# Cluster attention and spatial gating on one core: for batches 1 to 3 the mean of the values is formed on all partitions by one matmul and added by POOL, in place of flag and mean rows in the value product

## The chip, the cores and the metric

The kernel runs on one core of one Trainium2 chip. The metric is the device time of one execution in microseconds. The core has TensorE (PE in the profile, with its weight loads as PEld), VectorE (DVE), ScalarE (ACT), GpSimd (POOL), SyncE (SP, which here only issues DMAs), and 16 DMA engines. Each engine works through its own instructions in the order in which they were written out, and waits on semaphores for the others.

## The reference, cut to what matters

There are 4 batches, 8 heads, 768 positions, 64 elements a head and 16 clusters a head. Every query and key is given to the cluster whose centroid has the largest cosine with it; a query sees only the keys of its own cluster. A gated MLP follows that mixes over positions.

```python
mask = q_assign[:, :, :, None] == k_assign[:, :, None, :]
scores = scale * np.matmul(q, k.transpose(0, 1, 3, 2))
scores = np.where(mask, scores, -1000000000.0)
attn = np.exp(scores - np.max(scores, axis=-1, keepdims=True))
attn = attn / (np.sum(attn, axis=-1, keepdims=True) + 1e-09)
x = np.matmul(attn, v)                     # then heads side by side: (4, 768, 512)
h = np.maximum(x @ w_in, 0.0)              # w_in: 512 x 1024
u, v = h[..., :512], h[..., 512:]
v_n = (v - mean(v)) / np.sqrt(var(v) + 1e-06)
v_s = np.einsum('ts,bsd->btd', w_spatial, v_n) + b_spatial[None, :, None]
out = (u * v_s) @ w_out                    # w_out: 512 x 512
```

One case matters for this change: a query whose cluster holds no key. All its scores are then the same -1e9, its softmax is uniform, and its row of the output is the mean of all 768 values of that head.

## The kernel before, in words

Numbers that need more than one f16 are kept as a high and a low f16 part, so a product is made of three matmuls (high by high, high by low, low by high). Heads are treated in pairs: 4 batches of 4 pairs, so pair numbers n run from 0 to 15 and `NPR` is 4. The 768 positions are 6 tiles of 128.

`prep(n)` loads keys, queries and values of a pair, splits them (L527, L529 for queries and keys, L592, L593 for the values), finds the clusters (logits L544 to L546, then five DVE passes L557 to L562), and puts the one-hot rows of the clusters, scaled to a large penalty, under the queries and keys, so that the mask is part of the score matmul. It also forms the sum of the values over all positions: 12 matmuls with a matrix of ones (L600, L601) add the high and low parts of the six tiles, DVE takes the sum apart again into high and low (L609, L610), ACT scales the low part (L611), and two DMAs (L612, L613) put both as one row each (rows 81 and 82) into the tile `mean`.

`shifts(n)` computes the scores once to get each query's largest score (L641, reduced by DVE at L648), takes the negated maximum `nl` (L659), and lets ACT write three columns from it: the shift (L660) and two flag columns (L663), the second one scaled by a power of two. A flag is 1 for a query without a key in its cluster and 0 for the others. A DMA transpose (L664) and a DMA (L665) put the three as rows 80 to 82 under the queries.

`attend(n)` goes through two heads of six key tiles. For each key tile PE makes the scores (L685, L687), ACT the exponential (L691) and its high part (L693), POOL the low part (L694), and PE adds 18 matmuls of 65 or 64 columns to the accumulator `av` (L699). At the first key tile of a head six more matmuls go ahead of these: they multiply rows 0 to 82 of the queries with `mean`, so that flagged queries get the mean of the values, and the sum that belongs to it in column 64. Then DVE divides (L718 to L720, the result is `xn`), ACT makes the high part (L722), POOL the low part (L723), and a DMA transpose (L725) brings the pair to `xT`.

`mlp(b)` does the gated MLP of a batch: 324 matmuls of 128x512 a batch, all on one line (L743), with the normalisation on DVE and POOL (L764 to L785), gating (L804 to L806), a DMA transpose (L807) and the output. Its work is mixed with the attention of the batch behind it; the MLP of the last batch has no attention beside it.

The order of the work on each engine isn't written by hand. `Plan.run` simulates the engines once when the kernel is built: each operation carries an estimated duration, a due time (`DUE` for pairs of batch 0, `DUE_M` for later ones) and an offset to it (`K_SC`, `K_EXP` and the like), and the ready operation with the least due time plus offset goes next. Durations and offsets thus set only the order; the chip then takes its own time. Weights for the MLP are loaded and split in the same way (`weights`, L447 to L476), w_in early and w_spatial and w_out during batch 1.

## Time and profile before

| what | value |
|---|---|
| median of 3 runs | 699.76 us (699.73 to 700.55) |
| the profiled execution's own time | 698.77 us |
| its span, first to last instruction | 697.0 us |
| granted TensorE clock, mean | 0.998 |
| busy: PE, DVE, ACT, POOL | 637.2, 472.6, 434.7, 426.1 us |

A row of a grouping view reads: line, engine, operation, out<-in, shape, count | busy us, mean ns of one | idle us of the engine just before them, and what ended that idle time. A row of the waits reads: who waited for whom: us in total, times, longest us. A row of the table by stretches gives each engine's busy time in that stretch with its count of instructions. The time of an execution is a little longer than the span, which runs from the first to the last instruction.

### The profile page before, as it was taken

The numbers are of one execution on the slowest core, as the hardware profiler recorded it, in microseconds if no ns is written. First come the engines' busy times: TensorE is split into PE (matmuls) and PEld (weight loads), VectorE is DVE, ScalarE is ACT, GpSimd is POOL, SyncE is SP. The second block draws the span as 40 slices with busy tenths as digits, with TensorE's granted clock in tenths as the row PEclk, the third lists the DMA queues.
The fourth block names the chain that finished last, engine by engine and source line by source line (L and its number), as shares of the span: only waits on it lengthen the run. The fifth ranks groups of instructions, "written<-read, shape, count | busy, mean of one in ns | idle before, by whom it ended". The sixth has DMA issues, their size and how long they took to land.

```text
span 697.0 us, 16953 instructions
## 1 busy us (share of the span) xinstructions
PE 637.2 (91%) x6871; PEld 382.3 (55%) x6871; DVE 472.6 (68%) x933; ACT 434.7 (62%) x679; POOL 426.1 (61%) x296
## 2 busy tenths in 40 slices
PE   2578879989998898999999999999989999999997
PEld 1246656666546555566555656566555656544443
DVE  6989899996898989648687846748586732115220
ACT  2349999998587837569565956769465766612111
POOL 1027979988777936568557866658456857723311
PEclk9999999999999999999999999999999999999999
DMA  5475745676534675255421538345221123230123
GB/s 163 129 178 126 223 104 135 153 130 145 150 80 134 133 162 141 53 159 107 138 52 25 142 69 167 71 97 94 58 52 25 36 44 54 62 84 1 31 60 91
DMA packets 107322, 70.71 MB, mean 101 GB/s; under 512 B 91182, under 2 KB 93932, under 8 KB 107244
## 3 DMA queue, kind: packets, MB, share of 16 engines
...
q14 instruction: 24, 0.20, 0.1%
...
## 4 chain that ended last, share of the span: by engine, by line
PE 51%; DVE 23%; ACT 7%; DMA 7%; issue 5%; POOL 5%; SPq 1%; POOLq 0%; ACTq 0%; DVEq 0%
PE acc L743 30%; DVE nm L648 11%; PE acc L699 8%; PE sc L687 4%; PE sc L685 4%; PE acc L641 3%; POOL pt L694 3%; ACT p L691 3%; DMA gT<-ghl 2%; ACT pt L693 2%; DVE lo L529 1%; DVE y L778 1%; DVE v L783 1%; DMA raw<-in_kqT_dram 1%; DVE wsp L457 1%
## 5 line engine op out<-in xcount | busy, mean ns | idle before, releaser
L694 POOL TENSOR_TENSOR pt<-p,pt 128x768 f16<-128x768 f32 x192 | 327.8, 1722 | 123.6 <-ACT pt L693 91.7
L691 ACT ACTIVATE p<-sc,plog 128x768 f32<-128x768 f32 x192 | 169.0, 897 | 59.8 <-PE sc L687 51.7
L648 DVE TENSOR_REDUCE nm<-acc 128x1 f32<-128x512 f32 (+1 forms) x288 | 179.8, 683 | 4.4 <-PE acc L641 4.2
L693 ACT CAST pt<-p 128x768 f16<-128x768 f32 x192 | 156.0, 828 | 10.1 <-PE acc L699 8.3
L699 PEld LDWEIGHTS <-pt 128*128 128x128 f16 x3456 | 125.7, 98 | 33.4 <-POOL pt L694 8.1
L699 PE MATMUL acc<-vhl,pt 128*128 128x65 f16 (+1 forms) x3456 | 135.3, 194 | 6.6 <-POOL pt L694 6.4
L743 PE MATMUL acc<-win,xT 128*128 128x512 f16 x576 | 129.7, 379 | 0.3 <-DVE nm L648 0.2
L641 PE MATMUL acc<-hq 80*128 80x256 f16 (+1 forms) x384 | 101.3, 339 | 17.4 <-DVE nm L648 12.7
L685 PE MATMUL sc<-hq,lo 128*128 128x512 f16 (+1 forms) x384 | 95.8, 331 | 3.8 <-ACT p L691 3.6
L687 PE MATMUL sc<-hq 81*128 81x512 f16 (+1 forms) x384 | 96.0, 331 | 1.3 <-DMA hq<-sht 1.3
L743 PE MATMUL acc<-vn,wsp 128*128 128x512 f16 x432 | 97.0, 379 | 0.0
L743 PEld LDWEIGHTS <-xT 128*128 128x128 f16 x576 | 55.1, 98 | 63.3 <-issue 0.6
L806 POOL TENSOR_TENSOR ghl<-u,ghl 128x512 f16<-128x512 f32 x24 | 28.0, 1165 | 67.2 <-DVE ghl L805 53.3
L804 DVE SCALAR_TENSOR_TENSOR u<-acc,bsp,u 128x512 f32<-128x512 f32 x24 | 18.0, 748 | 75.3 <-PE acc L743 75.3
L743 PEld LDWEIGHTS <-wsp 128*128 128x128 f16 x432 | 41.9, 98 | 48.9
L743 PE MATMUL acc<-wou,gT 128*128 128x512 f16 x288 | 65.6, 379 | 3.3 <-DMA gT<-ghl 3.3
L529 DVE SCALAR_TENSOR_TENSOR lo<-raw,hq 128x768 f16<-128x768 f32 x32 | 42.6, 1337 | 25.4 <-ACT hq L527 25.3
L641 PEld LDWEIGHTS <-hq 80*128 80x128 f16 x384 | 34.0, 99 | 40.1 <-issue 21.1
L687 PEld LDWEIGHTS <-hq 81*128 81x128 f16 x384 | 37.9, 99 | 28.0 <-issue 3.2
L770 DVE BATCH_NORM_STATS2 st<-v 128x6 f32<-128x512 f32 x24 | 16.6, 694 | 47.2 <-ACT v L764 47.2
L685 PEld LDWEIGHTS <-lo 128*128 128x128 f16 x384 | 33.6, 98 | 25.9 <-issue 12.1
L743 PEld LDWEIGHTS <-gT 128*128 128x128 f16 x288 | 27.5, 98 | 35.6 <-DMA gT<-ghl 4.4
...
## 6 DMA issues: line engine op xcount, KB each, us to landing
...
```

The source lines that it names most:

```text
L529: los.append(op("DVE", 1.4 if n else 0.96, lambda h=h: V.scalar_tensor_tensor(out=lo.t[:, h, :], in0=raw.t[:, h, :], scalar=QK_SCALE, in1= ...
L641: T.matmul(out=acc.t[:, c:c + cs.stop - cs.start], lhsT=hq.t[0:R_SH, 1, h, t * P:(t + 1) * P], rhs=hq.t[0:R_SH, 0, h, cs], start=c == 0, s ...
L648: V.tensor_reduce(out=nm.t[:, t, k:k + 1] if n == 1 else nm.t[:, t:t + n, k], in_=src, axis=AX.X, op=ALU.max, negate=True)
L685: T.matmul(out=sc.t[:, cs], lhsT=lo.t[:, h, ks], rhs=hq.t[:, 2, h, cs], start=True, stop=False)
L687: T.matmul(out=sc.t[:, cs], lhsT=hq.t[0:R_E, 0, h, ks], rhs=hq.t[0:R_E, 1, h, cs], start=False, stop=True)
L691: o = op("ACT", 0.9, lambda sc=sc, p32=p32: A.activation(out=p32.t, in_=sc.t[:, 0:S], func=AF.Exp, bias=plog, scale=SC_UNIT), after=[o, m_ ...
L693: o = op("ACT", 0.83, lambda pt=pt, p32=p32: A.copy(out=pt.t[:, 0, :], in_=p32.t), after=[o], use=[p32], new=[pt], key=K_HI)
L694: o = op("POOL", 1.7, lambda pt=pt, p32=p32: G_.tensor_tensor(out=pt.t[:, 1, :], in0=p32.t, in1=pt.t[:, 0, :], op=ALU.subtract), after=[o] ...
L699: T.matmul(out=av.t[:, t * (D + 1):t * (D + 1) + w], lhsT=lhsT, rhs=rhs, skip_group_check=True, **f)
L743: T.matmul(out=acc.t, lhsT=lr[m][0], rhs=lr[m][1], start=(m == 0), stop=(m == n - 1))
L804: o = op("DVE", 0.72, lambda: V.scalar_tensor_tensor(out=u32.t, in0=acc.t, scalar=bsp[:, t:t + 1], in1=u32.t, op0=ALU.add, op1=ALU.mult), ...
L806: l = op("POOL", 1.2, lambda: G_.tensor_tensor(out=ghl.t[:, 1, :], in0=u32.t, in1=ghl.t[:, 0, :], op=ALU.subtract), after=[h], use=[u32, g ...
```

## The change

For n >= 4 (the pairs of batches 1 to 3) the mean of the values no longer goes through the value product. In `prep`, one DVE reduction sums the six tiles of the raw f32 values (128x768 to 128x128), one f32 matmul with a matrix of ones gives the sum over all partitions on every partition, and ACT copies it, scaled, to `m32`. The 12 matmuls, the two DVE operations, the ACT operation and the two DMAs of the mean rows are gone for these pairs. In `shifts`, the two flag columns are not written; one f32 flag a query, `fl`, is made instead. In `attend`, the six matmuls at the head's first key tile are gone, POOL forms flag times mean (`fm`, 128x384) ahead of time, and POOL adds it to `xn` between the division and ACT's copy. Pairs 0 to 3 keep the old way. Beside this, estimated durations and offsets of the plan are changed, so the order of operations on every engine can differ everywhere; `W_AT`, `W_GAP`, `WL_AT` and `WL_GAP` set the earliest times of the weights' loads. The description of the change says that its order was held under varied durations.

```diff
-DUE = 25.0
+DUE = 24.74
-DUE_M = 36.0
+DUE_M = 35.41
...
-W_KEY = 5.31
-WL_KEY = 2.39
-WL_AT = 182.62
-WL_GAP = 3.25
-W_AT = 30.25
-W_GAP = 5.6
-PREP_KEY = 2.04
+W_KEY = 5.99
+WL_KEY = 3.63
+WL_AT = 183.27
+WL_GAP = 0.47
+W_AT = 29.41
+W_GAP = 6.5
+PREP_KEY = 2.2
 AV_KEY = 1.61
-K_SC = -2.52
-K_MX = -2.84
-K_MAX = 0.11
+K_SC = -4.69
+K_MX = -2.73
+K_MAX = -0.03
...
-K_SH = -4.96
-K_EXP = 0.78
-K_HI = -1.47
-K_LO = 0.81
-K_RC = -1.0
-K_XD = 3.21
-K_X = -1.98
-K_VT = -4.0
-K_G = -3.19
+K_SH = -4.43
+K_EXP = 1.9
+K_HI = -2.11
+K_LO = 0.78
+K_RC = -1.03
+K_XD = 2.5
+K_X = -1.83
+K_VT = -0.74
+K_G = -3.88
...
+    whs = [const.tile([2, 2, D + 2], F16, name="wh%d" % i) for i in range(2)]
+    wls = [const.tile([2, 2, D + 2], F16, name="wl%d" % i) for i in range(2)]
+    one32 = const.tile([P, P], F32, name="one32")
...
-    r_wh = R(sm, "wh", [2, 2, D + 2], F16, 2)
+    r_wh = R(None, "wh", None, None, 2, tiles=whs)
+    r_vs = R(sm, "vs", [P, 2 * D], F32, 1)
+    r_m32 = R(sm, "m32", [P, 2 * D], F32, 2)
+    r_fl = R(sm, "fl", [P, NT], F32, 3)
+    r_fm = R(sm, "fm", [P, NT, D], F32, 1)
     r_w32 = R(sm, "w32", [2, 2, D + 2], F32, 1)
-    r_wl = R(sm, "wl", [2, 2, D + 2], F16, 2)
+    r_wl = R(None, "wl", None, None, 2, tiles=wls)
...
+    c_wh = op("POOL", 0.5, lambda: (G_.memset(one32, 1.0), [G_.memset(x[:, :, D:D + 1], S * MEAN_UNIT) for x in whs], [G_.memset(x[:, :, D:D + 1], 0.0) for x in wls]), key=-5)
...
-                lo = op("DVE", 0.05 + 0.00125 * n, lambda: V.scalar_tensor_tensor(out=dst()[:, 1, :], in0=x(), scalar=sc, in1=dst()[:, 0, :], op0=ALU.mult, op1=ALU.subtract), after=[h], use=use, key=key)
+                lo = op("DVE", (0.05 if n > 384 else 0.4) + 0.00125 * n, lambda: V.scalar_tensor_tensor(out=dst()[:, 1, :], in0=x(), scalar=sc, in1=dst()[:, 0, :], op0=ALU.mult, op1=ALU.subtract), after=[h], use=use, key=key)
...
-            x2 = op("DVE", 0.05 + 0.00125 * n, lambda raw=raw, top=top, n=n: V.scalar_tensor_tensor(out=top.t.bitcast(U32), in0=words(raw, n, 1), scalar=0xC0000000, in1=top.t.bitcast(U32), op0=ALU.bitwise_and, op1=ALU.bitwise_or), after=[x1], use=[raw, top], key=key)
-            x3 = op("DVE", 0.05 + 0.00125 * n, lambda raw=raw, top=top, n=n: V.scalar_tensor_tensor(out=top.t.bitcast(U32), in0=words(raw, n, 0), scalar=29, in1=top.t.bitcast(U32), op0=ALU.logical_shift_right, op1=ALU.bitwise_or), after=[x2], use=[raw, top], key=key)
+            x2 = op("DVE", (0.05 if n > 256 else 0.35) + 0.00125 * n, lambda raw=raw, top=top, n=n: V.scalar_tensor_tensor(out=top.t.bitcast(U32), in0=words(raw, n, 1), scalar=0xC0000000, in1=top.t.bitcast(U32), op0=ALU.bitwise_and, op1=ALU.bitwise_or), after=[x1], use=[raw, top], key=key)
+            x3 = op("DVE", (0.05 if n > 256 else 0.35) + 0.00125 * n, lambda raw=raw, top=top, n=n: V.scalar_tensor_tensor(out=top.t.bitcast(U32), in0=words(raw, n, 0), scalar=29, in1=top.t.bitcast(U32), op0=ALU.logical_shift_right, op1=ALU.bitwise_or), after=[x2], use=[raw, top], key=key)
...
-        hq, lo, vh, mw = r_hq.new(), r_lo.new(), r_vhl.new(), r_mean.new()
-        X.update(hq=hq, lo=lo, vhl=vh, mean=mw)
+        hq, lo, vh = r_hq.new(), r_lo.new(), r_vhl.new()
+        X.update(hq=hq, lo=lo, vhl=vh)
...
-        o = op("PE", 0.75, sums, after=[o_vh, o_vl, c_wt], use=[vh], new=[sv], cols=1548, key=KV)
-        wh, w32, wl = r_wh.new(), r_w32.new(), r_wl.new()
-
-        def svr():
-            return sv.t[0:2, 0:2 * (D + 2)].rearrange("p (h d) -> p h d", h=2)[:, :, 0:D + 1]
-
-        h_ = op("DVE", 0.25, lambda: V.tensor_scalar(out=wh.t[:, :, 0:D + 1], in0=svr(), scalar1=MEAN_UNIT, scalar2=None, op0=ALU.mult), after=[o], use=[sv], new=[wh], key=KV)
-        l_ = op("DVE", 0.3, lambda: V.scalar_tensor_tensor(out=w32.t[:, :, 0:D + 1], in0=svr(), scalar=MEAN_UNIT, in1=wh.t[:, :, 0:D + 1], op0=ALU.mult, op1=ALU.subtract), after=[h_], use=[sv, wh], new=[w32], key=KV)
-        l_ = op("ACT", 0.28, lambda: A.activation(out=wl.t[:, :, 0:D + 1], in_=w32.t[:, :, 0:D + 1], func=AF.Copy, scale=2.0 ** MEAN_LOG), after=[l_], use=[w32], new=[wl], key=KV)
-        w1 = sp(lambda: nc.sync.dma_start(out=mw.t[R_E:R_E + 1, :, 0:D + 1], in_=wh.t[0:1, :, 0:D + 1]), 0.05, after=[h_, c_mean], use=[wh], new=[mw], key=KV)
-        w2 = sp(lambda: nc.sync.dma_start(out=mw.t[R_E + 1:R_E + 2, :, 0:D + 1], in_=wl.t[0:1, :, 0:D + 1]), 0.05, after=[l_, c_mean], use=[wl, mw], key=KV)
+        short = n >= NPR
+        m, unit = D + 1, MEAN_UNIT
+        if short:
+            vs = r_vs.new()
+            o = op("DVE", 0.9, lambda: V.tensor_reduce(out=vs.t, in_=vraw.t.rearrange("p t c -> p c t"), axis=AX.X, op=ALU.add), after=[ldv], use=[vraw], new=[vs], key=KV)
+            o = op("PE", 0.4, lambda: T.matmul(out=sv.t[:, 0:2 * D], lhsT=one32, rhs=vs.t, start=True, stop=True), after=[o, c_wh], use=[vs], new=[sv], cols=512, key=KV)
+            m32 = X["m32"] = r_m32.new()
+            X["mo"] = op("ACT", 0.28, lambda: A.activation(out=m32.t, in_=sv.t[:, 0:2 * D], func=AF.Copy, scale=2.0 ** X_LOG / S), after=[o], use=[sv], new=[m32], key=KV)
+        else:
+            o = op("PE", 0.75, sums, after=[o_vh, o_vl, c_wt], use=[vh], new=[sv], cols=1548, key=KV)
+        X["mean"] = mw = None if short else r_mean.new()
+        if not short:
+            wh, w32, wl = r_wh.new(), r_w32.new(), r_wl.new()
+
+            def svr():
+                return sv.t[0:2, 0:2 * (D + 2)].rearrange("p (h d) -> p h d", h=2)[:, :, 0:m]
+
+            h_ = op("DVE", 0.25, lambda: V.tensor_scalar(out=wh.t[:, :, 0:m], in0=svr(), scalar1=unit, scalar2=None, op0=ALU.mult), after=[o, c_wh], use=[sv], new=[wh], key=KV)
+            l_ = op("DVE", 0.3, lambda: V.scalar_tensor_tensor(out=w32.t[:, :, 0:m], in0=svr(), scalar=unit, in1=wh.t[:, :, 0:m], op0=ALU.mult, op1=ALU.subtract), after=[h_], use=[sv, wh], new=[w32], key=KV)
+            l_ = op("ACT", 0.28, lambda: A.activation(out=wl.t[:, :, 0:m], in_=w32.t[:, :, 0:m], func=AF.Copy, scale=2.0 ** MEAN_LOG), after=[l_], use=[w32], new=[wl], key=KV)
+            w1 = sp(lambda: nc.sync.dma_start(out=mw.t[R_E:R_E + 1, :, 0:D + 1], in_=wh.t[0:1, :, 0:D + 1]), 0.05, after=[h_, c_mean], use=[wh], new=[mw], key=KV)
+            w2 = sp(lambda: nc.sync.dma_start(out=mw.t[R_E + 1:R_E + 2, :, 0:D + 1], in_=wl.t[0:1, :, 0:D + 1]), 0.05, after=[l_, c_mean], use=[wl, mw], key=KV)
         X["rows"] = rows + qa0
         X["go"] = rows + qa0 + [qa1, lo1]
-        X["v"] = [o_vh, o_vl, w1, w2]
+        X["v"] = [o_vh, o_vl] + ([] if short else [w1, w2])
...
+            if n >= NPR:
+                fl = r_fl.new()
+                o = op("ACT", 0.31, lambda nl=nl, fl=fl: A.activation(out=fl.t, in_=nl.t, func=AF.Relu, bias=flag[:, 0:1], scale=2 / LIM), after=[o, m_half], use=[nl], new=[fl], key=K_SH)
+                X.setdefault("fl", []).append((fl, o))
+            for c in range(2) if n < NPR else ():
                 u = 2.0 ** (-MEAN_LOG * c)
-                cols.append(op("ACT", 0.27, lambda nl=nl, sx=sx, c=c, u=u: A.activation(out=sx.t[:, :, R_E + c], in_=nl.t, func=AF.Relu, bias=flag[:, c:c + 1], scale=2 * u / LIM), after=[o, c_sh, m_half], use=[nl, sx], key=K_SH))
+                cols.append(op("ACT", 0.31, lambda nl=nl, sx=sx, c=c, u=u: A.activation(out=sx.t[:, :, R_E + c], in_=nl.t, func=AF.Relu, bias=flag[:, c:c + 1], scale=2 * u / LIM), after=[o, c_sh, m_half], use=[nl, sx], key=K_SH))
...
-                        if k == 0:
+                        if k == 0 and mw:
...
-                        mm(t, D + 1, pt.t[:, 0, ts], vh.t[:, k, h, 0:D + 1], start=False, stop=False)
+                        mm(t, D + 1, pt.t[:, 0, ts], vh.t[:, k, h, 0:D + 1], start=mw is None and k == 0 and t == 0, stop=False)
...
-                prev = op("PE", 0.56 + (0.19 if k == 0 else 0), values, after=[o, prev] + X["v"] + (xread.get(b - 2, []) if k == 0 else []), use=[pt, vh, mw] + ([av] if k else [hq]), new=[] if k else [av], cols=18 * 65, key=AV_KEY)
+                prev = op("PE", 0.56 + (0.19 if k == 0 and mw else 0), values, after=[o, prev] + X["v"] + (xread.get(b - 2, []) if k == 0 else []), use=[pt, vh] + ([mw] if mw else []) + ([av] if k else [hq] if mw else []), new=[] if k else [av], cols=18 * 65, key=AV_KEY)
...
+            if not mw:
+                fl, fo = X["fl"][h]
+                fm = r_fm.new()
+                f_ = op("POOL", 1.0, lambda fl=fl, fm=fm, hs=hs: G_.tensor_tensor(out=fm.t, in0=fl.t.unsqueeze(2).broadcast_to([P, NT, D]), in1=X["m32"].t[:, hs].unsqueeze(1).broadcast_to([P, NT, D]), op=ALU.mult), after=[fo, X["mo"]], use=[fl, X["m32"]], new=[fm], key=1.0)
+                o = op("POOL", 1.0, lambda xn=xn, fm=fm: G_.tensor_tensor(out=xn.t, in0=xn.t, in1=fm.t, op=ALU.add), after=[o, f_], use=[xn, fm], key=K_X)
             o = op("ACT", 0.5, lambda xn=xn, hs=hs: A.copy(out=xhl.t[:, :, 0, hs], in_=xn.t), after=[o], use=[xn] + ([xhl] if h else []), new=[] if h else [xhl], key=K_X)
```

More of the change, by code (lines that the diff above doesn't have):

```diff
@@ L470, in words @@
                 return raw.t[:, :2 * n].bitcast(U32).rearrange("p (n w) -> p n w", w=2)[:, :, k]
-            x1 = op("DVE", 0.1 + 0.0011 * n, lambda raw=raw, top=top, n=n: V.tensor_scalar(out=top.t.bitcast(U32), in0=words(raw, n, 1), scalar1=3, scalar2=0x3FFFFFFF, op0=ALU.logical_shift_left, op1=ALU.bitwise_and), after=[ld], use=[raw], new=[top], key=key)
-            x2 = op("DVE", 0.05 + 0.00125 * n, lambda raw=raw, top=top, n=n: V.scalar_tensor_tensor(out=top.t.bitcast(U32), in0=words(raw, n, 1), scalar=0xC0000000, in1=top.t.bitcast(U32), op0=ALU.bitwise_and, op1=ALU.bitwise_or), after=[x1], use=[raw, top], key=key)
-            x3 = op("DVE", 0.05 + 0.00125 * n, lambda raw=raw, top=top, n=n: V.scalar_tensor_tensor(out=top.t.bitcast(U32), in0=words(raw, n, 0), scalar=29, in1=top.t.bitcast(U32), op0=ALU.logical_shift_right, op1=ALU.bitwise_or), after=[x2], use=[raw, top], key=key)
+            x1 = op("DVE", (0.1 if n > 256 else 0.3) + 0.0011 * n, lambda raw=raw, top=top, n=n: V.tensor_scalar(out=top.t.bitcast(U32), in0=words(raw, n, 1), scalar1=3, scalar2=0x3FFFFFFF, op0=ALU.logical_shift_left, op1=ALU.bitwise_and), after=[ld], use=[raw], new=[top], key=key)
+            x2 = op("DVE", (0.05 if n > 256 else 0.35) + 0.00125 * n, lambda raw=raw, top=top, n=n: V.scalar_tensor_tensor(out=top.t.bitcast(U32), in0=words(raw, n, 1), scalar=0xC0000000, in1=top.t.bitcast(U32), op0=ALU.bitwise_and, op1=ALU.bitwise_or), after=[x1], use=[raw, top], key=key)
+            x3 = op("DVE", (0.05 if n > 256 else 0.35) + 0.00125 * n, lambda raw=raw, top=top, n=n: V.scalar_tensor_tensor(out=top.t.bitcast(U32), in0=words(raw, n, 0), scalar=29, in1=top.t.bitcast(U32), op0=ALU.logical_shift_right, op1=ALU.bitwise_or), after=[x2], use=[raw, top], key=key)
             lows(lambda top=top: top.t, [x3], use=[top])
@@ L520, in prep @@
         if n == 0:
-            raws = [move(("SP", "ACT")[h], lambda q, h=h: q.dma_start(out=raw.t[:, h, :], in_=kqT[b, p, :, h, :]), use=[raw] if h else [], new=[] if h else [raw], dma=2.2, key=KP) for h in range(2)]
+            raws = [move(("SP", "ACT")[h], lambda q, h=h: q.dma_start(out=raw.t[:, h, :], in_=kqT[b, p, :, h, :]), use=[raw] if h else [], new=[] if h else [raw], dma=1.8, key=KP) for h in range(2)]
         else:
@@ L648, in most @@
                     V.tensor_reduce(out=nm.t[:, t, k:k + 1] if n == 1 else nm.t[:, t:t + n, k], in_=src, axis=AX.X, op=ALU.max, negate=True)
-                tops.append(op("DVE", 0.65, most, after=[o], use=[acc] + ([nm] if tops else []), new=[] if tops else [nm], key=K_MAX))
+                tops.append(op("DVE", 0.68, most, after=[o], use=[acc] + ([nm] if tops else []), new=[] if tops else [nm], key=K_MAX))
             for t in range(0, NT, 2):
@@ L693, in attend @@
                 o = op("ACT", 0.83, lambda pt=pt, p32=p32: A.copy(out=pt.t[:, 0, :], in_=p32.t), after=[o], use=[p32], new=[pt], key=K_HI)
-                o = op("POOL", 1.7, lambda pt=pt, p32=p32: G_.tensor_tensor(out=pt.t[:, 1, :], in0=p32.t, in1=pt.t[:, 0, :], op=ALU.subtract), after=[o], use=[p32, pt], key=K_LO)
+                o = op("POOL", 1.72, lambda pt=pt, p32=p32: G_.tensor_tensor(out=pt.t[:, 1, :], in0=p32.t, in1=pt.t[:, 0, :], op=ALU.subtract), after=[o], use=[p32, pt], key=K_LO)
                 def values(av=av, pt=pt, h=h, k=k):
```

1 line of the change is left out of this document (removed).

## The prediction

> **What bounds the kernel now.** I read the page's first part for the busiest engine, then the chain that ended last for what set the end, then a table by stretches, since the shares are averages over unlike stages, and last the waits of PE.
>
> ```profile
> span 697.0 us, 16953 instructions
> PE 637.2 (91%) x6871; PEld 382.3 (55%) x6871; DVE 472.6 (68%) x933; ACT 434.7 (62%) x679; POOL 426.1 (61%) x296
> PE 51%; DVE 23%; ACT 7%; DMA 7%; issue 5%; POOL 5%; SPq 1%; POOLq 0%; ACTq 0%; DVEq 0%
> ...
> 45.00:145.00 100.00, 89.30 (x1328) 63.29 (x1327) 93.56 (x174) 93.86 (x148) 86.14 (x53) 0.98 0.63 150
> 145.00:290.00 145.00, 133.10 (x1523) 81.97 (x1522) 127.92 (x240) 106.45 (x174) 105.95 (x68) 1.00 0.54 126
> 290.00:612.00 322.00, 316.75 (x3485) 191.70 (x3484) 193.12 (x368) 209.70 (x317) 213.30 (x148) 1.00 0.37 81
> 612.00:697.00 85.00, 78.57 (x378) 35.33 (x374) 20.93 (x55) 13.05 (x22) 18.01 (x17) 1.00 0.20 55
> ```
>
> The last four lines are stretches of the span: length, then busy time of PE, PEld, DVE, ACT and POOL, the granted clock, the DMA share and GB/s. From 45 to 145 us (batch 0) DVE and ACT are both at 94% and no engine alone is the bound. From 145 to 290 us, where the late weights are split beside the attention, PE has 92% and DVE 88%. From 290 to 612 us PE has 316.75 of 322 us: it alone is the bound, and DVE (60%), ACT (65%) and POOL (66%) have room. From 612 us on only the last MLP is left. The narrower stretch below shows that within the second stage DVE comes first for a while, 65.85 of 70 us, and the waits show that PE's largest loss is on DVE, which empties the accumulators of the maximum scores (L648).
>
> ```profile
> 215.00:285.00 70.00, 62.22 (x744) 38.97 (x743) 65.85 (x114) 47.47 (x79) 48.03 (x30) 1.00 0.58 138
> ```
> ```profile
> PE acc L641 <- DVE nm L648: 12.7, 23, 1.4
> PE acc L699 <- POOL pt L694: 6.4, 12, 1.1
> PE acc L601 <- DVE vhl L593: 3.0, 4, 1.0
> ```
>
> **The change part by part.** PE first. The 12 matmuls of the value sum run from the first row below to the start of the next operation; a value group of 24 with its six mean matmuls stands beside one of 18 in the chain of waits:
>
> ```profile
> 548.62 0.22 PE L600 MATMUL acc<-vhl,ones 128*128 128x130 f16 x1
> 548.68 0.22 PE L601 MATMUL acc<-vhl,ones 128*128 128x128 f16 x1
> ...
> 549.32 0.22 PE L699 MATMUL acc<-vhl,pt 128*128 128x65 f16 x2
> ...
> 329.22 1.27 PE acc L699 x42
> 333.08 1.09 PE acc L699 x36
> ```
>
> So a pair loses 549.32 - 548.62 = 0.70 us of PE in `prep`, and 1.27 - 1.09 = 0.18 us a head, 0.36 us a pair, in `attend`. It gains one f32 matmul of 128 columns. The only f32 matmul of the trace is the transposition of the centroids:
>
> ```profile
> L426 PE MATMUL acc<-p 128*128 128x128 f32 x1 | 0.5, 476 | 6.6 <-DVE p L423 6.6
> ```
>
> The f16 matmul of the same shape lasts 0.22 us and holds PE for the 0.06 us to the next. With f32's 476 ns as latency, the extra 0.25 us on top of 0.06 makes 0.31 us, which I take; the ends are 0.06 us (as f16) and 0.48 us (nothing overlaps). By the Trainium skill, FP8 and Floating Point Precision, TensorE Precision Notes, a true f32 product goes four times through the array, which would make four times the 0.06 us spacing, an estimate of 0.23 us, and the whole sum about 0.9 us better over 11 pairs; no row here has f32 matmuls back to back. By my value a pair saves 0.70 + 0.36 - 0.31 = 0.75 us of PE.
>
> DVE and ACT. Removed are L609, L610, L611 and four of L663 (two a head, of which one a head comes back as `fl`):
>
> ```profile
> L609 DVE TENSOR_SCALAR wh<-acc 2x130 f16<-2x130 f32 x16 | 4.4, 276 | 4.8 <-PE acc L601 4.8
> L610 DVE SCALAR_TENSOR_TENSOR w<-acc,wh 2x130 f32<-2x130 f32 x16 | 4.4, 275 | 0.2
> L611 ACT ACTIVATE wl<-w 2x130 f16<-2x130 f32 x16 | 4.9, 308 | 20.6 <-DVE w L610 20.1 <-ACT o L814 0.4
> L663 ACT ACTIVATE shx<-nl,flag 128x6 f16<-128x6 f32 x64 | 15.9, 307 | 0.0
> L648 DVE TENSOR_REDUCE nm<-acc 128x1 f32<-128x512 f32 (+1 forms) x288 | 179.8, 683 | 4.4 <-PE acc L641 4.2
> L529 DVE SCALAR_TENSOR_TENSOR lo<-raw,hq x32: 910/970/2393, 8.4 to 461.2; 128x768 f16<-128x768 f32 x32
> ```
>
> The added reduction reads 768 f32 elements a partition. At the rate of L648 (512 in 683 ns, from PSUM) it takes 1.02 us, at the shortest 768-element pass (L529, 910 ns) 0.91; its strided view is not in the trace, and at two steps an element it would be 2.0. I take 0.97, by the nearer rows. A pair then adds 0.97 - 0.55 = 0.42 us to DVE. ACT loses 0.31 + 4 x 0.31 and gets 2 x 0.31 and a copy of 128x128, about 0.30 between L663's 307 ns for 6 elements and less than 0.6 for the 512 of other copies: 0.6 us less a pair. ACT is the bound nowhere, so that is worth nothing; cover gone (45 to 145 us) it would win at most 0.6.
>
> POOL gets two operations a head on 128x384 f32. Its one operation of that size, and the ones beside it:
>
> ```profile
> L723 POOL TENSOR_TENSOR xhl<-xn,xhl x32: 904/913/1632, 65.8 to 614.2; 128x384 f16<-128x384 f32 x32
> L694 POOL TENSOR_TENSOR pt<-p,pt x192: 1632/1642/2968, 46.5 to 609.7; 128x768 f16<-128x768 f32 x192
> ...
> L806 POOL TENSOR_TENSOR ghl<-u,ghl 128x512 f16<-128x512 f32 x24 | 28.0, 1165 | 67.2 <-DVE ghl L805 53.3 <-DVE rc L718 4.1 <-PE acc L743 3.8
> ```
>
> I take 0.95 us, between L723's 0.91 and L806's 1.165 for a third more; operands that are broadcast are not in the trace on POOL, so 0.91 to 1.17 stay as ends. That is 3.8 us a pair, 24 x 1.9 = 46 us in all. From 290 to 612 us it makes POOL's 213 us 213 + 17 x 1.9 = 246 of 322, so it is covered there by idle time. The price is contention: median and maximum of L529 and L694 lie far apart, and in the timeline one sees DVE operations of 0.55 to 0.97 us take 2 us while POOL runs back to back:
>
> ```profile
> 215.54 2.00 DVE L529 SCALAR_TENSOR_TENSOR lo<-raw,hq 128x768 f16<-128x768 f32 x1 [0.32 <-ACT hq L527]
> 217.47 1.99 DVE L457 SCALAR_TENSOR_TENSOR wsp<-wraw,wsp 128x384 f16<-128x384 f32 x1
> 219.01 3.31 POOL L785 TENSOR_TENSOR vn<-v,vn 128x512 f16<-128x512 f32 x2
> ```
>
> L529's mean (42.6 us by 32, 1.34 us) is 0.43 above its shortest while POOL is busy 61% of the span. The added 46 us lift POOL by some 10 points over 467 us, so an exposed DVE operation loses 0.07 us more, and with some ten a pair DVE pays 0.7 us a pair, an estimate. The Trainium skill, SBUF — State Buffer, Who interferes with whom, says that a `tensor_reduce` never contends with GpSimd while operations with two SBUF inputs do; L529 agrees (two inputs, 2.39 us at worst) and L648 reads PSUM and so can't tell. If the rule failed for the new reduction, it would lose 0.43 us like L529, 5 us of DVE over 12 pairs, mostly in cover.
>
> SP loses two DMAs a pair. It goes through its issues in order, and L612 held what stood behind it for 24.8 us in four waits (the row below), L664's transposes among them. Also the shift column is ready after one ACT operation and not three, 0.61 us sooner. What PE waits for these rows is 1.3 us in all (the second row), so I take 0, with 1.3 us of gain as the other end.
>
> ```profile
> SPq L612 <- DVE w L610: 24.8, 4, 18.6
> ...
> PE sc L687 <- DMA hq<-sht: 1.3, 1, 1.3
> ```
>
> The sums' wait for `vhl` (3.0 us above) goes, as the f32 matmul needs only the raw values and the reduction; a wait on that reduction may take its place. I take 1 of it. In the end of the run the added POOL step makes `xn` 0.95 us later: L723 ended at 614.24 + 0.91 = 615.15 us, SP's transpose of it began at 616.51 behind one that ran from 615.18 for 1.23 us:
>
> ```profile
> 614.24 0.91 POOL L723 TENSOR_TENSOR xhl<-xn,xhl 128x384 f16<-128x384 f32 x1 [0.80 <-ACT xhl L722]
> 615.18 1.23 SPq L807 DMA_TRANSPOSE gT<-ghl  x1
> 616.51 2.01 SPq L725 DMA_TRANSPOSE xT<-xhl  x1
> ```
>
> 615.15 + 0.95 = 616.10 is still before 616.51, so this costs nothing; with that cover gone, up to 0.95.
>
> The order is new on all engines. The old plan held a split of 256 columns (L457, L474) at 0.37 us, and the new one at 0.72 and 0.67; the rows have 733 and 797 ns, so the plan now is nearer to the chip in the stage where DVE comes first.
>
> ```profile
> L457 DVE SCALAR_TENSOR_TENSOR wou<-top,wou 128x256 f16<-128x256 f32 x8 | 5.9, 733 | 1.0 <-ACT wou L456 1.0
> L474 DVE SCALAR_TENSOR_TENSOR top<-wraw,top 128x256 uint32<-128x256 uint32 x8 | 6.4, 797 | 0.2
> ```
>
> What order can win is bounded by PE's waits on DVE, 12.7 us; it can lose as much. I take 0.
>
> **The sum by stage.** L600 has 6 instructions a pair:
>
> ```profile
> 145.00:290.00 145.00, 3.54 (x24) 2.30 (x24) 1.00 0.54 126
> 290.00:612.00 322.00, 5.64 (x42) 4.03 (x42) 1.00 0.37 81
> ```
>
> So four preparations of changed pairs fall in 145 to 290, seven in 290 to 612, and one before; of the 24 heads I count 7 and 17, since the first changed pair is attended after 145. From 290 to 612: 7 x (0.70 - 0.31) + 17 x 0.18 = 5.8 us of PE; a tenth off for the places where the chain runs through DVE leaves 5.2. From 145 to 290: PE saves 4 x 0.39 + 7 x 0.18 = 2.8 us, of which half (1.4) counts, outside 215 to 285; there DVE pays about 1.5 pairs x (0.42 + 0.7) = 1.7. Net +0.3. Before 145: one preparation, ACT lighter and DVE heavier, 0. The `vhl` wait: -1. The sum is 0.3 - 5.2 - 1 = -5.9, on the profiled execution's 698.77 us: 692.9. The median of the runs is 0.99 us above that execution, so I forecast 693.8.
>
> **The rivals.** (a) POOL's queue takes the gain and more: slower. The addition waits for DVE's `xn` and stands in POOL's order ahead of the low parts (L694) that PE needs next. It delays them by 0.95 us and the wait before it, about 0.24 (below, 7.8 us by 32): 1.19 us a head.
>
> ```profile
> L723 POOL TENSOR_TENSOR xhl<-xn,xhl 128x384 f16<-128x384 f32 x32 | 31.3, 977 | 7.8 <-ACT xhl L722 7.5
> ```
>
> It decides from the point where more than (5.9 + 1.4) / 1.19 = 6 of 24 heads pass the delay on to PE. For it: PE waits 6.4 us on L694 already, and a DVE operation hit by POOL makes `xn` later still. Against it: four `pt` buffers lie between, and POOL is idle 109 us from 290 to 612. With 8 heads it gives 699.76 - 5.9 + 9.5 = 703.4. (b) DVE takes the place of PE for longer: its 12 x 1.1 = 13 us land in the second stage and in the pieces of L648 between, nearly half of it (5.9) shows, and the time stays at 699.8. For it: DVE has 23% of the chain; against it: 129 us idle from 290 to 612. (c) The cut counts in full and the nearer plan wins a third of the 12.7 us: 699.76 - 9.0 - 4.2 = 686.6. That the change doesn't remove the work can't be: the matmuls are not issued for n >= 4.
>
> **How the numbers follow.** My case has 0.52, (a) 0.20, (b) 0.12, (c) 0.16. Measurement tells 0.2%, 1.4 us, from no change: faster 0.52 + 0.16 = 0.68, same 0.12, slower 0.20. My case alone runs from 689.1 to 697.7: the f32 matmul -2.8 to +1.9, SP's rows -1.3, the tenth taken off -0.6, POOL's upper price +1 where it is not covered, the tail +0.95. For 8 in 10 the range goes from 686.0, which leaves out the far half of (c), to 703.5, which leaves out the worse half of (a).
>
> **What would show it.** Right: PE's busy time from 290 to the last attention falls by about 6 us at nearly full PE; f32 matmul rows near 0.3 us; the reduction near 0.97 us with a narrow spread; POOL at some 470 us with its two new rows near 0.95. Wrong: a row of PE waiting on L694 well over 6.4 us points to (a), one of L641 on L648 well over 12.7 us to (b), and PE idle at places where the order differs and no new operation stands points to the plan.

## The result, and the profile after

The changed kernel takes 723.2 us (median; 720.7 to 725.2) against 699.98 us before: a ratio of 1.0354, with an interval of 1.0317 to 1.0391. It is 3.5% slower, 24.8 us at 700 us. I had forecast 693.8, and my range ended at 703.5.

First the page's first part, and the chain that ended last, of the changed kernel:

```profile
span 718.9 us, 16364 instructions
PE 638.5 (89%) x6607; PEld 377.2 (52%) x6607; DVE 502.0 (70%) x921; ACT 431.8 (60%) x655; POOL 475.6 (66%) x349
PE 43%; DVE 34%; POOL 8%; issue 7%; DMA 5%; ACT 4%; SPq 0%; POOLq 0%; DVEq 0%; ACTq 0%
```

PE issues 264 matmuls less and yet is busy as long as before (638.5 against 637.2 us). DVE rises by 29 us, POOL by 50, and in the chain PE falls from 51 to 43%, DVE rises from 23 to 34% and POOL from 5 to 8%. The table by stretches (length; busy time of PE, PEld, DVE, ACT, POOL; granted clock; DMA share; GB/s):

```profile
45.00:145.00 100.00, 85.85 (x1326) 60.27 (x1325) 99.01 (x173) 92.95 (x147) 87.39 (x55) 1.00 0.66 150
145.00:290.00 145.00, 129.44 (x1401) 79.32 (x1399) 127.00 (x216) 100.47 (x155) 111.32 (x77) 0.94 0.50 123
290.00:612.00 322.00, 303.79 (x3131) 179.82 (x3129) 213.93 (x374) 199.77 (x297) 238.12 (x173) 0.96 0.37 78
612.00:719.00 107.00, 98.94 (x587) 47.24 (x585) 24.77 (x61) 26.18 (x39) 35.77 (x30) 1.00 0.24 53
```

In the stretch from 290 to 612 us, where I took PE for the only bound, PE now gets through 3131 instructions in place of 3485, has 18 us idle in place of 5, and its granted clock is 0.96 in place of 1.00. About 170 of the 354 missing instructions are the removed matmuls themselves (7 x 10 + 17 x 6, by the prediction's counts); the rest is work that comes later. In the profiled execution of the kernel before, the half clock showed once; the mean clock of the changed kernel's span is 0.971, so (1 - 0.971) x 2 x 718.9 = 42 us passed at half clock. The clock of the kernel before is not the same in each execution: in the 66 that ran beside the experiments its mean was 0.985 to 1.000, by the same sum 0 to 21 us at half clock; in the changed kernel's four it was 0.967 to 0.971. The new operations, and PE's waits:

```profile
L615 DVE TENSOR_REDUCE vs<-vraw 128x128 f32<-128x768 f32 x12 | 18.0, 1500 | 0.0
L616 PE MATMUL acc<-vs,one 128*128 128x128 f32 x24 | 5.2, 300 | 1.0 <-DVE vs L615 0.8 <-DVE nm L667 0.2
L749 POOL TENSOR_TENSOR xn<-xn,fm 128x384 f32<-128x384 f32 x24 | 32.8, 1368 | 12.9 <-DVE xn L743 12.4 <-ACT fl L682 0.4
L748 POOL TENSOR_TENSOR fm<-fl,m 128x384 f32<-128x384 f32 x24 | 23.0, 959 | 0.6
...
PE acc L660 <- DVE nm L667: 20.4, 23, 4.8
PE acc L771 <- DMA gT<-ghl: 8.3, 4, 2.3
...
PE acc L722 <- POOL pt L717: 5.0, 7, 1.5
```

The reduction takes 1.50 us and not 0.97. PE's wait for the maximum scores (L667, the L648 of before) grew from 12.7 to 20.4 us, and its longest from 1.4 to 4.8 us. Its wait for POOL's low parts (L717, the L694 of before) did not grow: 5.0 us, where it was 6.4. The longest wait, in the timeline:

```profile
369.94 0.49 PE L710 MATMUL sc<-hq 81*128 81x512 f16 x2
...
370.26 0.72 PE L722 MATMUL acc<-vhl,pt 128*128 128x65 f16 x18
370.28 0.69 POOL L805 TENSOR_TENSOR y<-a,mhalf 128x2 f32<-128x2 f32 x1 [3.08 <-DVE a L804]
...
370.94 3.23 POOL L717 TENSOR_TENSOR pt<-p,pt 128x768 f16<-128x768 f32 x2
371.00 1.59 DVE L806 TENSOR_TENSOR y<-y 128x2 f32<-128x2 f32 x1 [0.81 <-POOL y L805]
...
372.63 1.56 DVE L807 TENSOR_TENSOR y<-y,a 128x2 f32<-128x2 f32 x1
...
375.08 2.48 DVE L667 TENSOR_REDUCE nm<-acc 128x1 f32<-128x512 f32 x4
375.82 0.58 PE L660 MATMUL acc<-hq 80*128 80x512 f16 x1 [4.83 <-DVE nm L667]
...
376.20 0.84 PE L708 MATMUL sc<-hq,lo 128*128 128x512 f16 x2
```

DVE is late. POOL waits 3.08 us for it at L805, with two low parts (L717) behind in its queue. Once POOL goes on, it runs these two while DVE does its own operations on two elements, which take 1.59 and 1.56 us where the shortest of each take 0.16. The maximum that PE needs comes last, and two score matmuls, which took 0.49 us before the wait, take 0.84 after it. The same stretch by windows, before the wait, in it and behind it:

```profile
366.60:370.10 3.50, 3.50 (x36) 2.11 (x34) 3.33 (x9) 2.06 (x3) 0.60 (x1) 1.00 0.14 28
370.10:373.50 3.40, 0.88 (x20) 0.71 (x19) 2.56 (x3) 2.01 (x3) 3.22 (x3) 1.00 0.18 37
373.50:383.80 10.30, 7.98 (x40) 4.21 (x40) 7.22 (x13) 3.60 (x5) 2.80 (x3) 0.50 0.04 10
```

A 3.4 us window in which PE was busy for 0.88 us is followed by 10.3 us at a clock of 0.50.

### The profile page after: what moved, and what is told of

Its sections match the earlier page's. It is cut to its first block, busy times and chain, and to the rows that moved or that the text cites. A ratio compares the mean times of both kernels' runs of the same rounds, so it can differ in the third digit from the quotient of the medians.

```text
span 718.9 us, 16364 instructions
## 1 busy us (share of the span) xinstructions
PE 638.5 (89%) x6607; PEld 377.2 (52%) x6607; DVE 502.0 (70%) x921; ACT 431.8 (60%) x655; POOL 475.6 (66%) x349
## 4 chain that ended last, share of the span: by engine, by line
PE 43%; DVE 34%; POOL 8%; issue 7%; DMA 5%; ACT 4%; SPq 0%; POOLq 0%; DVEq 0%; ACTq 0%
PE acc L771 27%; DVE nm L667 14%; PE acc L722 5%; POOL pt L717 3%; PE sc L708 3%; PE sc L710 3%; DMA gT<-ghl 3%; PE acc L660 3%; DVE lo L537 2%; DVE vhl L601 1%; POOL xn L749 1%; POOL vn L813 1%; DVE y L806 1%; DVE v L811 1%; DVE wsp L465 1%
## 5 line engine op out<-in xcount | busy, mean ns | idle before, releaser
L717 POOL TENSOR_TENSOR pt<-p,pt 128x768 f16<-128x768 f32 x192 | 323.2, 1697 | 108.1 <-ACT pt L716 74.5
L667 DVE TENSOR_REDUCE nm<-acc 128x1 f32<-128x512 f32 (+1 forms) x288 | 179.7, 683 | 18.0 <-PE acc L660 17.6
L722 PEld LDWEIGHTS <-pt 128*128 128x128 f16 x3456 | 129.2, 99 | 37.2 <-issue 11.0
L660 PE MATMUL acc<-hq 80*128 80x256 f16 (+1 forms) x384 | 102.9, 349 | 26.2 <-DVE nm L667 20.4
L708 PE MATMUL sc<-hq,lo 128*128 128x512 f16 (+1 forms) x384 | 99.2, 341 | 3.4 <-ACT p L714 2.5
L710 PE MATMUL sc<-hq 81*128 81x512 f16 (+1 forms) x384 | 99.1, 340 | 1.3 <-DMA hq<-sht 1.2
L771 PE MATMUL acc<-wou,gT 128*128 128x512 f16 x288 | 67.3, 385 | 9.1 <-DMA gT<-ghl 8.3
L660 PEld LDWEIGHTS <-hq 80*128 80x128 f16 x384 | 35.7, 101 | 43.4 <-issue 22.7
L537 DVE SCALAR_TENSOR_TENSOR lo<-raw,hq 128x768 f16<-128x768 f32 x32 | 44.2, 1384 | 2.3 <-ACT hq L535 2.2
```

The costliest lines, as they stand in the source:

```text
L537: los.append(op("DVE", 1.4 if n else 0.96, lambda h=h: V.scalar_tensor_tensor(out=lo.t[:, h, :], in0=raw.t[:, h, :], scalar=QK_SCALE, in1= ...
L660: T.matmul(out=acc.t[:, c:c + cs.stop - cs.start], lhsT=hq.t[0:R_SH, 1, h, t * P:(t + 1) * P], rhs=hq.t[0:R_SH, 0, h, cs], start=c == 0, s ...
L667: V.tensor_reduce(out=nm.t[:, t, k:k + 1] if n == 1 else nm.t[:, t:t + n, k], in_=src, axis=AX.X, op=ALU.max, negate=True)
L708: T.matmul(out=sc.t[:, cs], lhsT=lo.t[:, h, ks], rhs=hq.t[:, 2, h, cs], start=True, stop=False)
L710: T.matmul(out=sc.t[:, cs], lhsT=hq.t[0:R_E, 0, h, ks], rhs=hq.t[0:R_E, 1, h, cs], start=False, stop=True)
L717: o = op("POOL", 1.72, lambda pt=pt, p32=p32: G_.tensor_tensor(out=pt.t[:, 1, :], in0=p32.t, in1=pt.t[:, 0, :], op=ALU.subtract), after=[o ...
```

## The experiments

The median of the kernel before moved between 697.4 and 700.6 us from one set of runs to another, so ratios to it are compared. Where a time is compared with a forecast, it is the ratio times 699.98 us. Theory A says that the new operations' load on DVE and POOL, and the waits that it makes, is the loss; theory B that the new constants give a worse order whatever the operations. Where an edit leaves the order of all engines' instructions as it was, "same order" says so.

**Operations or plan.** e1 has the new operations under the old constants and estimates of the plan, e2 the old operations under the new ones.

```diff
 # e1, in the changed kernel (all plan constants and old estimates back)
-DUE = 24.74
+DUE = 25.0
...
 # e2, in the kernel before (all plan constants and new estimates in)
-DUE = 25.0
+DUE = 24.74
```

> The changed kernel's operations with all constants and estimated durations of the plan as they were before (the new operations keep their own estimates). Theory A, the new operations' durations on the chip (a reduction of 1.50 us for a planned 0.9, POOL's 46 us that stretch DVE) break any order: 712 to 722 us, with several stretches at half clock. Theory B, the new parameters give a worse order whatever the operations: 692 to 701 us, with the one half-clock stretch that the kernel before has.

> The kernel before with the changed kernel's constants and estimated durations, no new operation. Theory A: 697 to 703 us, since no duration has changed. Theory B: 710 to 722 us, with half-clock stretches behind PE's waits on L648 as in the changed kernel.

Measured: e1 1.0198 (1.0161 to 1.0234), e2 1.0034 (1.0005 to 1.0063). The plan alone costs 0.3%, so theory B falls as I put it; the operations alone cost 2.0%, as theory A has it. But both together cost more than the sum: under the new operations the new plan is another 1.5% worse than the old one, so the order has a part in the 3.5% too.

**The two durations, in the same order.** e3 shortens the reduction, e4 POOL's two operations, e5 both.

```diff
 # e3
-V.tensor_reduce(out=vs.t, in_=vraw.t.rearrange("p t c -> p c t"), axis=AX.X ...
+V.tensor_reduce(out=vs.t, in_=vraw.t.rearrange("p t c -> p c t")[:, :, 0:2], axis=AX.X ...
 # e4
-G_.tensor_tensor(out=xn.t, in0=xn.t, in1=fm.t, op=ALU.add)
+G_.tensor_tensor(out=xn.t[:, :, 0:1], in0=xn.t[:, :, 0:1], in1=fm.t[:, :, 0:1], op=ALU.add)
...
```

> The changed kernel, where the reduction of the raw values takes in two of the six tiles only (so the mean leaves out four tiles); the plan's estimate stays, so the order on every engine is the same. The reduction falls from 1.50 to about 0.5 us, 12 us of DVE in all. Theory A: 706 to 714 us and fewer half-clock stretches, the 5 us wait of PE at 370 us down to 3 to 4. Theory B: not over 4 us faster, 718 to 724.

> The changed kernel, where POOL's two new operations work on one element of 64 (so the mean is added to one column only); the plan's estimates stay and so does the order. POOL loses about 35 of its 46 us. Theory A, contention: 706 to 715 us, DVE's total for the short y operations and the splits down by 5 us or more. Theory B: 718 to 724.

> The changed kernel in its own order, with both shortenings together: the reduction takes in two of six tiles, and POOL's two new operations one element of 64 (the mean leaves out four tiles and is added to one column). PE's saving stays in. If the two durations are the whole loss and add up, 723 - 15 - 17 = 691 us and half-clock time back to about 4 us; if both hit the same waits, 700 to 706.

Measured: e3 1.0110 (1.0053 to 1.0168), e4 1.0113 (1.0044 to 1.0183), e5 0.9943 (0.9913 to 0.9973). Each takes off 2.4 points of the 3.5, both 4.1. With these intervals that is not told apart from 4.8, the sum of the two; e5 comes out at 696.0 us, between my 691 and my 700 to 706, so whether both hit the same waits stays open. With most of both out, the order of the change is 0.6% faster than before, 4.0 us: that is what is left of the saving when most of the added load is gone. So the two loads make the loss in this order. PE's wait for the maxima in e3, e4 and e5, then its wait for the low parts in e4 and a line of e4's page:

```profile
PE acc L660 <- DVE nm L667: 13.9, 24, 2.4
...
PE acc L660 <- DVE nm L667: 16.4, 25, 3.1
...
PE acc L660 <- DVE nm L667: 9.0, 20, 1.3
...
PE acc L722 <- POOL pt L717: 1.0, 2, 0.6
...
PE 633.7 (90%) x6607; PEld 375.7 (53%) x6607; DVE 488.9 (70%) x921; ACT 430.3 (61%) x655; POOL 439.8 (63%) x349
```

e4 shortens operations of POOL alone, yet DVE is busy 488.9 us in place of 502.0, 13.1 us less, and PE waits 4.0 us less for DVE's maxima. PE's wait for the low parts falls by as much, from 5.0 to 1.0 us. So in the changed kernel POOL's new operations cost time in two ways: they make DVE's operations slower, and they delay the low parts in POOL's queue. How much of the loss each makes isn't told apart.

**What the half clock costs.** e6 puts useless matmuls right ahead of four of PE's long waits; the order is otherwise the same.

```diff
-... values, after=[o, prev] + ...
+... lambda values=values, av=av, pt=pt, c={(3, 1, 2): 36, (8, 0, 3): 44, (9, 0, 3): 90, (13, 0, 3): 90}.get((n, h, k), 0): (values(), [T.matmul(out=av.t[:, 390:512], lhsT=pt.t[:, 0, 0:P], rhs=pt.t[:, 0, 0:122], start=False, stop=False, skip_group_check=True) for _ in range(c)]), after=[o, prev] + ...
```

> The changed kernel in its own order, with 260 matmuls of 122 columns (about 13 us of PE work) added that write accumulator columns nobody reads, put right ahead of four of PE's long waits (near 142, 320, 371 and 531 us: 36, 44, 90 and 90 of them). If a long idle time of PE costs a second time through the half clock that follows it, four half-clock stretches of 27 us in all go and the time falls by 6 to 13 us, to 710 to 717, although work was added. If the half clock is a mere accompaniment, 722 to 727.

Measured: 1.0260 (1.0218 to 1.0302), 0.9 points or 6.6 us below the changed kernel, although 260 matmuls more are issued; that is the low end of the 6 to 13 us that I forecast. The mean granted clock rises from 0.971 to 0.983, which by the sum above is 24 us at half clock in place of 42. The place of the 4.83 us wait, and the two windows behind its start, in e6:

```profile
370.06 4.96 PE L734 MATMUL acc<-pt 128*128 128x122 f16 x90
375.08 0.38 PE L660 MATMUL acc<-hq 80*128 80x512 f16 x1
375.30 0.49 PE L708 MATMUL sc<-hq,lo 128*128 128x512 f16 x2
...
370.00:373.40 3.40, 3.40 (x71) 3.40 (x68) 3.12 (x2) 1.44 (x2) 3.40 (x3) 1.00 0.06 16
373.40:383.60 10.20, 10.14 (x110) 6.72 (x108) 10.10 (x21) 7.06 (x11) 4.47 (x4) 1.00 0.13 26
```

The maximum comes 0.7 us earlier here (375.08 against 375.82 us), and PE goes on at full clock: 110 instructions in the 10.2 us from 373.40 us on, of which 31 are useless ones, so 79 of the kernel's own where the changed kernel had 40. So a wait of PE is paid a second time through the clock.

**Better estimates, another sum.** e7 tells the plan the durations that the chip took. e8 takes the sum from the 12 f16 matmuls of before, whose result stands on all partitions anyway, and drops the reduction and the f32 matmul; e9 is the same under the old plan.

```diff
 # e7
-o = op("DVE", 0.9, lambda: V.tensor_reduce(out=vs.t, ...
+o = op("DVE", 1.5, lambda: V.tensor_reduce(out=vs.t, ...
-o = op("POOL", 1.0, lambda xn=xn, fm=fm: ...
+o = op("POOL", 1.4, lambda xn=xn, fm=fm: ...
 # e8, e9
-vs = r_vs.new()
-o = op("DVE", 0.9, lambda: V.tensor_reduce(...
-o = op("PE", 0.4, lambda: T.matmul(out=sv.t[:, 0:2 * D], lhsT=one32, rhs=vs.t, ...
+o = op("PE", 0.75, sums, after=[o_vh, o_vl, c_wt], use=[vh], new=[sv], cols=1548, key=KV)
...
```

> The changed kernel, with the plan's estimates of the reduction (0.9) and of POOL's addition (1.0) set to what the chip took (1.5 and 1.4), so the order is made anew. If the loss comes from an order made for durations that the chip doesn't keep, 704 to 714 us; if from the load itself, 718 to 726.

> The changed kernel without the reduction and the f32 matmul: the 12 f16 matmuls of before make the sum, which stands on all partitions, and ACT copies it to the mean; POOL's part stays. DVE loses 1.5 us a pair against the changed kernel, PE gets 0.5 us a pair back. By the loss from the reduction (15 us in the same order) less 12 x 0.5 us: 712 to 716 us. The order is made anew, so 705 to 722 are open.

> As the run with the f16 sum, but with the plan's constants and estimates of before: of the new work only POOL's two operations a head stay, and PE keeps 0.36 us a pair of its saving (4.3 us in all). If POOL's load alone costs some 12 us here too: 703 to 712; if the order made by the new constants was the worse part: 694 to 699, faster than before.

Measured: e7 1.0412 (1.0362 to 1.0463), e8 1.0087 (1.0055 to 1.0119), e9 1.0208 (1.0172 to 1.0244). Setting these two estimates right doesn't mend it; e7 is one more new order, so that some other order would suit the new operations is not excluded. e8 is 2.7 points better than the changed kernel, more than the 1.0 to 1.6 I expected from the reduction, and it makes PE's work larger. e9, which keeps only POOL's part, is 2.1% slower than before, against my 694 to 699 for a good old plan and above the 703 to 712 for POOL's load. It is no faster than e1 (2.0%), which has the reduction as well: under the old plan the reduction's cost doesn't show, under the new one it is 2.4 to 2.7 points. What a load costs depends on the order that it stands in.

**Each cost by itself, in the old order.** e10 to e12 change the kernel before and keep its order: a useless reduction, useless POOL additions, and less PE work.

```diff
 # e10, behind L593, pairs from 4 on
+n >= NPR and V.tensor_reduce(out=wst, in_=vraw.t.rearrange("p t c -> p c t"), axis=AX.X, op=ALU.add)
 # e11, behind L723, pairs from 4 on
+n >= NPR and [G_.tensor_tensor(out=wst, in0=xn.t, in1=xn.t, op=ALU.add) for _ in range(2)]
 # e12
-for t in range(NT):
+for t in range(NT) if n < NPR else (0, NT - 1):
...
-if k == 0:
+if k == 0 and (n < NPR or t == 0):
```

> The kernel before, in its own order, with one useless reduction of the raw values (L615's form, 1.5 us) behind L593 of every pair from 4 on; 18 us of DVE in all. By the prediction's cover (DVE idle for 129 us from 290 to 612) 699 to 703 us. By theory A, in-order waits of PE behind DVE and half clock after them: 707 to 715.

> The kernel before, in its own order, with two useless POOL additions of 128x384 f32 behind L723 of every head of pairs from 4 on, 48 operations, some 45 us of POOL. By the prediction's cover (POOL idle for 109 us from 290 to 612) 699 to 703 us; by theory A, contention with DVE and late low parts: 705 to 714, with the means of DVE's two-input operations up.

> The kernel before, in its own order, with less PE work for pairs from 4 on and nothing else: 3 of the 12 sum matmuls stay and 1 of the 6 mean matmuls a head (the mean leaves out four tiles and five of six query tiles). PE loses 9 x 0.058 + 10 x 0.03 = 0.82 us a pair, 9.8 us in all. If PE is the bound that the prediction took it for: 692 to 695 us. If the waits only grow by what PE saves: 697 to 700.

Measured: e10 1.0134 (1.0093 to 1.0176), 9.4 us for 18 us of DVE; e11 1.0252 (1.0213 to 1.0291), 17.6 us for 40.3 us of POOL, above both forecasts; e12 0.9993 (0.9966 to 1.0019), 0.5 us for 9.8 us of PE. These three make 9.4 + 17.6 - 0.5 = 26.5 us; the change measured 24.8. That the two are alike is no proof that the parts are the whole: the same operations cost 13.9 us under the old constants (e1), and the additions here stand behind L723 and not ahead of ACT's copy. In e10 PE's two largest waits don't grow (12.2 us for the maxima, 6.8 for the low parts); its waits for the divided values `xn` do, from 0.3 to 4.6 us. Where PE's saving went, from 290 to 612 us: first the table and the waits of e12, then the waits of the kernel before in the same stretch.

```profile
290.00:612.00 322.00, 312.40 (x3353) 186.44 (x3352) 193.02 (x370) 209.74 (x317) 214.21 (x148) 1.00 0.39 80
...
PE acc L699 <- POOL pt L694: 4.5, 9, 1.2
PE acc L641 <- DVE nm L648: 4.2, 4, 1.4
```

```profile
PE acc L641 <- DVE nm L648: 3.7, 4, 1.1
PE acc L743 <- DMA gT<-ghl: 0.5, 1, 0.5
PE acc L699 <- POOL pt L694: 0.4, 2, 0.2
```

PE is busy 4.4 us less and waits for POOL's low parts 4.5 us, where it was 0.4. In this stretch, what PE saves it spends on waiting for POOL. Over the whole run PE is busy 9.0 us less (628.2 against 637.2) and the two waits grow by 3.8 us; a part of the rest may be the clock, which was 0.983 to 0.997 in e12's executions and 0.988 to 0.997 in those of the kernel before beside them.

**Why POOL's time counts.** e13 replaces e11's additions by memsets (writes of a constant) of about the same length, which read nothing from SBUF, the on-chip memory of the tiles. e14 turns L694 into a copy (the low part of the exponentials is left out), e15 is e14 with the PE cut of e12. All three keep the old order.

```diff
 # e13
+n >= NPR and [G_.memset(wst, 0.0) for _ in range(2)]
 # e14, e15
-G_.tensor_tensor(out=pt.t[:, 1, :], in0=p32.t, in1=pt.t[:, 0, :], op=ALU.subtract)
+G_.tensor_copy(out=pt.t[:, 1, :], in_=pt.t[:, 0, :])
```

> The kernel before, in its own order, with two memsets of 128x960 f16 on POOL behind L723 of every head of pairs from 4 on, each about 0.93 us, in place of the useless additions: the same time in POOL's queue, nothing read from SBUF. If the loss of the useless additions (2.5%) is delay in the queue: again 2.0 to 2.7%, 712 to 718 us. If it is contention with DVE over SBUF: 0 to 0.6%, 698 to 703.

> The kernel before, in its own order, with L694 as a copy of the high part (the low part is left out of the computation), so that POOL's 327.8 us fall to some 150. If POOL's low parts pace the stage beside PE: 684 to 692 us. If PE is the bound: 696 to 699.

> The run before this one together with the cut of 9.8 us of PE work (3 of 12 sum matmuls, 1 of 6 mean matmuls a head for pairs from 4 on). If PE's saving was held up by POOL's low parts: 5 to 8 us below the run before this one. If DVE's reductions hold it as well: 0 to 3 us below.

Measured: e13 1.0302 (1.0246 to 1.0357), e14 0.9679 (0.9637 to 0.9720), e15 0.9639 (0.9594 to 0.9683). The memset rows and PE's waits of e13, then PE's first wait of e11, then the stretch from 290 to 612 us of e14:

```profile
L723 POOL MEMSET wst<- 128x960 f16 x48 | 43.4, 904 | 1.4
...
PE acc L699 <- POOL pt L694: 15.0, 20, 2.0
```

```profile
PE acc L699 <- POOL pt L694: 13.6, 18, 1.9
```

```profile
290.00:612.00 322.00, 320.23 (x3452) 192.40 (x3450) 178.38 (x381) 207.70 (x316) 131.33 (x147) 1.00 0.37 81
```

43 us of memsets cost 3.0%, at least as much as 40 us of additions, and PE's wait for low parts rises from 6.4 us to 13.6 in e11 and 15.0 in e13. So in this order the loss needs no added operation that reads SBUF: delay of the low parts in POOL's queue is one way to it. It is not the whole: the waits grow by 7 to 9 us of 17.6 and 21.1, DVE is busy 11.3 us longer in e11 and 7.7 in e13, and the clock in e13's executions was 0.976 to 0.983, where that of the kernel before beside them was 0.988 to 1.000. In the changed kernel this wait was no longer than before (5.0 us). With the 327.8 us of L694 down to 166.7 (e14) 22 us go, more than I forecast. DVE is busy 14.7 us less there too (178.38 against 193.12 us in the stretch), so e14 doesn't tell POOL's queue from POOL's effect on DVE. PE's cut is then worth 2.7 us of its 9.8 (e15; 677.2 to 674.5 us), within the 0 to 3 for DVE's reductions holding it as well. Even there most of it is not on the path.

**Trying to use it.** e16 to e18 let DVE make some of the low parts in the kernel before; the plan makes a new order.

```diff
-o = op("POOL", 1.7, lambda pt=pt, p32=p32: G_.tensor_tensor(...
+lo_dve = n >= 8 and k == 3          # e17: n >= 8 and k in (1, 4); e18: n >= 4 and k == 3
+o = op("DVE" if lo_dve else "POOL", 1.05 if lo_dve else 1.7, lambda pt=pt, p32=p32, e=V if lo_dve else G_: e.tensor_tensor(...
```

> The kernel before, with one of the six low parts (L694) of every head from pair 8 on made by DVE in place of POOL: POOL loses 16 x 1.7 = 27 us, DVE gains 16 us. Parameters of the plan as before, the order made anew. If POOL's queue is the pace (46 us of it cost 17 us): 690 to 697 us. If DVE's queue is as tight: 698 to 705.

> As the run before, two of six low parts from pair 8 on: POOL loses 54 us, DVE gains 32. If POOL's queue is the pace: 684 to 693 us. If DVE's queue is as tight: 700 to 710.

> One of six low parts a head on DVE from pair 4 on, through the stage where DVE is busy 88 to 94%: POOL loses 41 us, DVE gains 24. If POOL is the pace there too: 686 to 694 us. If DVE is: 697 to 706, above the first of these runs.

Measured: e16 0.9996 (0.9977 to 1.0015), e17 1.0375 (1.0345 to 1.0404), e18 1.0085 (1.0055 to 1.0115). None beats the kernel before; e16 and e18 lie in the ranges for DVE being as tight, e17 above its 700 to 710. In e17 PE waits on the maxima 52 times, against 23 times for 12.7 us before:

```profile
PE acc L641 <- DVE nm L648: 18.4, 52, 1.4
```

Work moved from POOL to DVE won nothing. Why isn't shown: how much of e17's loss comes from its new order and how much from DVE's load isn't told apart, and in e16 PE waits less than before on both, 9.6 us for the maxima and 3.9 for the low parts, with the time unchanged.

## Why the prediction was wrong

- **"It alone is the bound", and so POOL's and DVE's added work "is covered there by idle time".** This is the step that failed, and the sum stood on it. PE was busy 316.75 of 322 us from 290 to 612, but 9.8 us less work in the old order (e12) changed the time by -0.5 us, with an interval of -2.4 to +1.3. The cover is what made the change slower and not only useless: with both loads shortened in the same order (e5) the change gains 4.0 us, with them it loses 24.8. A busy share of 98% said that PE had little slack, not that the others had any: PE with less to do waited for POOL's low parts (e12), and half of L694's time gone won 22 us (e14). The chain had given a hint: PE's share of it was 51% of the span, where its busy share was 91%.
- **PE's saving.** Its size was right: the f32 matmul went out as two instructions, 5.2 us busy in all, 0.43 us a pair, within my ends of 0.06 and 0.48. In the old order it was worth next to nothing; in the order of the change all savings together, less the cost of what was left of the loads, came to 4.0 us (e5).
- **The reduction.** I took 0.97 us by the nearest rows and kept 2.0 as the far end for the strided view; it took 1.50. Worse was its weight: I charged 1.7 us in one stage and called the rest covered; 18 us of DVE cost 9.4 us in the old order (e10), and shortening the reduction in the order of the change takes 2.4 points off (e3).
- **POOL's operations.** 0.95 us was right for the product (0.96), and low for the addition (1.37, shortest 0.99). I costed 46 us of POOL at nothing in its own queue, naming as cover that POOL was idle 109 us from 290 to 612. The two took 32.8 + 23.0 = 55.8 us, and shortening them takes 2.4 points off (e4).
- **The rivals.** By my own signs it was rival (b), DVE: PE's wait for the maxima went from 12.7 to 20.4 us. The sign of (a), a wait on L694 well over 6.4 us, did not come (5.0 us, and 1.0 with POOL's new operations short), though e11 and e13 show that its mechanism, low parts delayed in POOL's queue, is there in the old order. I had (b) end at 699.8 us, since I took DVE's rise as 13 us; it was 29. I gave the two chances of 0.12 and 0.20, and neither time is near 723.2.
- **Contention.** This term was mis-sized. I put 0.7 us a pair on DVE, 8.4 us over 12 pairs. DVE rose by 29.4 us; 18.0 for the reduction less 12 x 0.55 = 6.6 for what was removed leaves 18 us of operations that took longer, such as L806 at 1.59 us, and 13.1 us go when POOL's operations alone are shortened (e4). That is one way in which POOL's work reached PE in the changed kernel. The trace agrees with the rule of the Trainium skill (SBUF — State Buffer, Who interferes with whom) that a `tensor_reduce` doesn't contend: twelve L615 took 1.48 to 1.54 us each, the one at 363.39 us 1.48 beside a POOL operation with two inputs.
- **The half clock.** There was no term for it. The row was in the trace of before, one stretch from 76.9 us, and I read the mean of 0.998 and went on. In the changed kernel 42 us passed at half clock; filling the waits ahead of four of these stretches won 6.6 us (e6).
- **Order.** I took 0. The new constants cost 0.3% on the old operations (e2) and 1.5% under the new ones (e1 against the changed kernel). That new estimates came nearer to the chip was no gain; e7, nearer still, is no faster.
- **Right:** SP's two DMAs less are worth nothing visible (PE waits 1.2 us for the rows under the queries, before 1.3; nothing tested them alone), and the POOL step at the end of the run stayed covered: its transpose starts 636.88 - 636.59 = 0.3 us after L751 ends.

```profile
635.68 0.91 POOL L751 TENSOR_TENSOR xhl<-xn,xhl 128x384 f16<-128x384 f32 x1 [0.62 <-ACT xhl L750]
636.88 2.46 SPq L753 DMA_TRANSPOSE xT<-xhl  x1
```
